# Normalised attention and a GELU layer on one core: batch 0's steps in another order and on other engines

## The chip, the cores and the metric

The kernel runs on one core of a Trainium2 chip. The metric is the device time of one execution in microseconds; the time before is the median of 3 runs. One further execution was profiled; its trace is what the views below are read from.

## The reference

q, k and v have 8 batches, 12 heads, 448 positions and 64 elements a head; the two weights are 768 x 2048 and 2048 x 768.

```
q_n = q / sqrt(mean(q*q) + 1e-6) * g_q;  k_n likewise with g_k
attn = softmax(q_n @ k_n.T / 8);  o = attn @ v
x = o, heads side by side: (8*448) x 768
h = x @ w_in;  g = gelu_tanh(h);  out = g @ w_out
```

## The kernel before

The kernel goes through the batches one after the other. While the attention of one batch runs, the second layer of the batch before it fills TensorE; the order of the later batches is written out in strings (STEPS, L641). The change touches only what comes ahead of these: the attention and the first layer of batch 0, mixed with the first steps of batch 1. That part is the string FRONT (L897), and `front` (L805) carries out its words one by one. The order of the words is the order of the instructions in each engine's queue: no scheduler moves them. An engine takes its instructions in that order and waits at each for what it needs, so a word that waits holds back every later word of the same engine, and of no other.

A word is a step, a number and, behind a colon, the engine: A ScalarE, D VectorE, P GpSimd. The heads are worked on in pairs; a chunk c is two pairs (hp 2c and 2c+1), three chunks make a batch. For batch 0 the number of the steps up to the copies is the pair.

- sq, sk: squares of the raw q or k of a pair (L175; q of 112 x 512, k of 128 x 384 for an even pair and 128 x 512 for an odd one). They are kept in the buffer that later holds g. tq, tk: their sums (L203, VectorE). rs, rS: the reciprocal root as a logarithm and an exponential (L206, ScalarE), for one pair or for both of a chunk.
- nq, nk: raw times reciprocal root, to bf16 (L220). tpq, tpk: transposes on TensorE into PSUM (L232). cq, ck: copies from there into qT and kT (L252, L258); ck multiplies by the gains, gcol.
- gcol, shift: the gains, and a bound that is taken off the scores ahead of the exponential (L780, L788).
- s: the scores of one tile (L301), of which a chunk has seven: three key blocks of the even pair, a tile "r" of the left-over keys of both pairs, three of the odd pair. e: its exponential (L332, ScalarE), which frees the PSUM place of the tile. There are two such places, and a third from U on, when the places of the transposes are given up. They are handed on first in, first out, and the "hh" tiles of the first layer take turns in the same three.
- sa, sb: the sums of a pair's exponentials by a matmul with ones, in two halves (tile o). st, rc, rb: their reciprocals (VectorE). xa, xb: exponentials times v (tile ox). xt: their product, xT (L399).
- mb, ma, mc, md: matmuls of the first layer (L504) by ranges of the six pairs; for ma to md the number i stands for columns 2i and 2i+1 of sixteen, for 7 and 8 for one column each. mb n takes pair n for columns 0 and 1, ma pairs 0 to 3, mc pair 4, md 0 to 2 pair 5, md from 3 on all six pairs. g: the GELU of a tile (L525), which frees its place.
- GELU, EXP: load of ScalarE's tables. y: matmuls of zeros, whose result nobody reads.
- L11, L12: loads of q and k of batch 1's chunks 1 and 2 on the SP queue. v, V: loads of v for batch 0 and 1; w: quarters of w_in; o: quarters of w_out. These go out on GpSimd's queue, whose DMAs take eight completion flags in turn, so that an issue waits for the landing of the eighth before it.
- Sq, Sk, Tq, Tk, Rs, Nq, Nk, Tp, Cq, Ck: the same first steps for batch 1, where Sq, Sk, Tq, Tk take a whole chunk (Sq2 is all of chunk 2's q, Sk2 its k), Rs0 makes the roots of chunks 0 and 1, and Nq01 is chunk 0, second pair. Tp0 and Tp1 transpose pairs 0 and 1 into the two single banks that the last two first-layer tiles (md7, md8) use too; pairs 2 and 3 follow behind FRONT.

Behind FRONT come the second layer of batch 0 (tiles o, mm, om; L432) and the attention of batch 1, both in the order of STEPS. Its second group of matmuls begins with the second half of w_out's columns.

The loads of q and k go out on SP's queue: three chunks of batch 0 and the first of batch 1 ahead of FRONT (L740 to L744), then L11 and L12.

Of the kernel before, what the change touches and what calls it, by code (L numbers as in the profile page):

```python
# [16 lines left out]
def kernel(  # L17
# [12 lines left out]
    B, H, S, D = q.shape  # L30
# [8 lines left out]
    P = 112  # L39
# [48 lines left out]
    gcol = consts.tile([128, 1], F32)  # L88
# [3 lines left out]
    shift = consts.tile([128, 1], F32)  # L92
# [189 lines left out]
    exs, exrs, ess, oas = {}, {}, {}, {}  # L282

    def place(name):
        i = unused.pop(0)
        t = spots[i].tile([128, 2, 512], F32, tag="sc", name=name)
        taken.append((t, i))
        return t

    def leave(t):  # L290

        n = next(n for n, (u, _) in enumerate(taken) if u is t)
        unused.append(taken.pop(n)[1])
# [7 lines left out]
    def scores(b, hp, t, parts=1):  # L301

        c, j = hp // 2, hp % 2
        sc = place("sc")
        if t == "r":
            exrs[b, c] = exr.tile([128, 2, S], BF16, tag="exr", name="exr")
            for a in range(2):
                for jj in range(2):
                    r = slice(a * D, (a + 1) * D)
                    o = slice(64 * jj, 64 * jj + 64)  # L310
                    nc.tensor.matmul(  # L311
                        sc[o, a, :S], kT[r, c, NK, o], qT[b][r, 2 * c + jj],
                        start=True, stop=True,
                    )
            dst = exrs[b, c]
        else:
            if t == 0:
                exs[b, hp] = exq.tile([128, NK, 2, S], BF16, tag="ex", name="ex")

            m = 128 // parts  # L320
            for a in range(2):
                r = slice(a * D, (a + 1) * D)
                for i in range(parts):
                    o = slice(i * m, i * m + m)
                    nc.tensor.matmul(  # L325
                        sc[o, a, :S], kT[r, c, 4 * j + t, o], qT[b][r, hp],
                        start=True, stop=True,
                    )
            dst = exs[b, hp][:, t]

        def exp():
            nc.scalar.activation(dst, sc[:, :, :S], AF.Exp, scale=scale, bias=shift)  # L332
            leave(sc)
        return exp
# [327 lines left out]
    def run(b, text, m2, call, after):  # L662

        w = work.setdefault(b, dict(n=0, a=0, but=(), k={}))
        for token in text.split():
# [5 lines left out]
            elif kind == "s":  # L671
                n = w["n"]
                if n % 3 == 0:
                    call("side", n // 3)
                scores(b, *(SEQ if n < 14 else LAST)[n], 2)()
                w["n"] += 1
                if n % 3 == 2:
# [127 lines left out]
    def front(step):  # L805
# [25 lines left out]
        elif name == "shift":  # L831
            shifts()
        elif name == "s":
            exps[i] = scores(0, *TILES[i])
        elif name == "e":
            exps[i]()
# [58 lines left out]
            raise ValueError(step)  # L895

    FRONT = """  # L897
        sk0:D v1 sq0:A tq0 tk0 rs0 gcol sk1:A sq1:D nq0:P v2 tq1 nk0:D tk1 rs1 sq2:A sk2:A tpq0
        y1 tpk0 v0 nq1:P ck0:D shift cq0:D s0 sq3:A e0 y3 s1 tq2 tq3 tk2 nk1:P L11 e1 y3 tpk1
        tpq1 s2 sk3:P w0 e2 ck1:D cq1:D tk3 y1 y1 s3 y3 y4 s4 sa0 rS1 nq2:P e3 sk4:A e4 sq4:D  # L900
        nk2:D s5 sb0 tpq2 s6 tpk2 tq4 tk4 st0 cq2:D rc0 ck2:D e5 sq5:P nk3:P nq3:D L12 e6 sa1 s7
        tpk3 tpq3 s8 sb1 e7 rs4 s9 xa0 sk5:P ck3:D rb0 cq3:D tk5 st1 e8 e9 xb0 s10 xt0 tq5 rc1
        rb1 nk4:P nq4:P e10 sa2 s11 rs5 e11 nk5:P nq5:P w1 xa1 sb2 xb1 s12 tpk4 tpq4 s13 Sq0:P
        Sk0:P e12 cq4:A st2 xt1 ck4:D rc2 rb2 e13 xa2 xb2 sa3 tpq5 tpk5 s14 e14 xt2 ck5:D cq5:D
        s15 xa3 sb3 e15 U xb3 s16 s17 s18 e16 st3 e17 rc3 rb3 xt3 e18 sa4 mb0 mb1 sb4 xa4 xb4
        s19 s20 Tq0 st4 rc4 rb4 sa5 mb2 Sk1:P w2 w3 e19 e20 GELU o0 Sq1:A xt4 Tk0 mb3 xa5 sb5
        xb5 ma1 mc0 mc1 st5 o1 V0 V1 rc5 rb5 xt5 Tq1 Tk1 Sk2:D md0 md1 ma2 mc2 md2 g0 g1 EXP md3
        Rs0 Nk00:D Nq01:D Nq00:D md4 Tp0 g2 g3 V2 o2 o3 Cq0:A g4 Nk01:D Ck0:A md5 Tp1 Nk11:D
        Nq11:D Nk10:D Nq10:D Sq2:D Tk2 Tq2 Ck1:A g5 Cq1:A md6 md7 g6 g7 md8 g8
"""  # L910
    for step in FRONT.split():
        front(step)
# [173 lines left out]
```

## Time and profile before

| | us |
|---|---|
| median of 3 runs | 407.01 (406.73 to 408.34) |
| the profiled execution | 404.76 |
| its span in the trace | 403.0 |
| TensorE busy | 392.5 (97%) |
| ScalarE busy | 304.6 (76%) |
| VectorE busy | 247.4 (61%) |
| GpSimd busy | 131.9 (33%) |

PE is TensorE, ACT ScalarE, DVE VectorE, POOL GpSimd, SP the queue that issues most DMAs. In the page's slices the span is cut into 40 of equal length, 10.1 us each; a digit is the busy share in tenths, 9 for nine tenths or more. A row of a timeline is: start, duration, engine, line, operation, written tile and read tiles with their shapes, how often; in brackets the idle time before it and what ended it. The duration of one instruction holds its way through the engine; several in a row stand closer than that, and the time of one is then the row's duration by the count. A row of DMA issues has the size and the time from issue to landing. The chain of work that ended last is followed back from the last instruction to what released it, and so on.

### The profile page before, as it was taken

Reading aid. Unit: us, or ns where it says so; the run is one execution under the profiler, and the core shown is the slowest. Engines: PE = TensorE matmul, PEld = TensorE weight load, DVE = VectorE, ACT = ScalarE, POOL = GpSimd, SP = SyncE. Lnnn points to the kernel's source line nnn. Section 1 sums busy time; section 2 is a strip of 40 time slices with the busy share of each in tenths; the row PEclk is TensorE's granted clock in tenths of the full one; section 3 lists DMA queues with packets and bytes.
Section 4 is the critical chain, followed back from the end, with each engine's and each line's share of the span. In section 5 each row is a group of like instructions: output and inputs, shape, how many; then the busy total and the mean of one; then the engine's idle time right before and its main releaser. Section 6 shows DMA issues by size and latency. Waiting matters only on the chain.

```text
span 403.0 us, 17090 instructions
## 1 busy us (share of the span) xinstructions
PE 392.5 (97%) x7632; PEld 271.7 (67%) x7632; DVE 247.4 (61%) x414; ACT 304.6 (76%) x412; POOL 131.9 (33%) x143
## 2 busy tenths in 40 slices
PE   6899999999999999999999999999999999999996
PEld 3444557667778897767867777666877667766564
DVE  5889839986987346963787426874587331880010
ACT  4997889969997689876997669876998548964400
POOL 6888000242500934065500735037500640000000
PEclk9999999999999999999999999999999999999999
DMA  7999999999990899339971399828780290210022
GB/s 186 219 227 229 205 197 200 214 251 166 214 180 3 180 190 199 76 86 199 197 127 40 78 195 191 144 53 182 135 136 15 76 144 3 81 42 2 3 78 79
DMA packets 97897, 54.64 MB, mean 136 GB/s; under 512 B 63776, under 2 KB 94368, under 8 KB 97824
## 3 DMA queue, kind: packets, MB, share of 16 engines
q1 hardware_dynamic: 71392, 41.69, 46.4%
q0 software_dynamic: 26112, 11.80, 23.1%
q8 instruction: 59, 0.97, 1.1%
q14 instruction: 14, 0.11, 0.1%
q10 hardware_dynamic: 320, 0.07, 0.1%
HBM read 45.61 MB, written 11.01 MB: 141 GB/s over the span
## 4 chain that ended last, share of the span: by engine, by line
PE 81%; DMA 6%; POOL 4%; DVE 4%; issue 2%; ACT 1%; SPq 1%; ACTq 0%; DVEq 0%; POOLq 0%
PE hh L432 23%; PE om L432 14%; PE o L432 10%; PE mm L432 10%; PE sc L325 6%; PE o L546 5%; PE hh L517 4%; PE so L432 4%; DMA vb<-in_v_dram 3%; POOL nrmq L227 1%; PE ox L371 1%; DMA rawq<-in_q_dram 1%; DVE es L346 1%; PE sc L311 1%; DMA kT<-nrmk 1%
## 5 line engine op out<-in xcount | busy, mean ns | idle before, releaser
L332 ACT ACTIVATE ex<-sc,shift 128x896 bf16<-128x896 f32 x144 | 137.7, 1016 | 8.6 <-PE sc L325 8.3
L432 PE MATMUL hh<-xT,win 64*64 64x448 bf16 x2304 | 131.7, 349 | 0.0
L432 PEld LDWEIGHTS <-g 64*64 64x64 bf16 x3072 | 103.0, 107 | 28.7 <-issue 2.2
L432 PEld LDWEIGHTS <-win 64*64 64x64 bf16 x2688 | 89.6, 107 | 37.1 <-ACTq L441 6.8
L432 PE MATMUL om<-wout,g 64*64 64x384 bf16 x1664 | 101.3, 323 | 0.2 <-issue 0.2
L432 PE MATMUL o<-wout,g 64*64 64x384 bf16 x704 | 83.4, 323 | 0.6 <-ACT g L526 0.6
L432 PE MATMUL mm<-wout,g 64*64 64x384 bf16 x704 | 83.5, 323 | 0.0
L204 DVE TENSOR_REDUCE ss<-sq 128x14 f32<-128x896 f32 (+4 forms) x45 | 47.9, 1080 | 45.4 <-ACT sq L187 37.9
L526 ACT ACTIVATE g<-hh 128x896 bf16<-128x896 f32 x55 | 49.7, 915 | 24.7 <-PE hh L432 22.8
L325 PE MATMUL sc<-qT,kT 64*64 64x448 bf16 (+1 forms) x540 | 53.7, 352 | 1.6 <-DVE qT L256 1.3
L926 POOL COPY mark<-es 1x1 bf16<-1x1 bf16 x8 | 1.8, 225 | 138.2 <-DVE xT L402 41.8
L227 POOL TENSOR_TENSOR nrmq<-rawq,rinv 112x512 bf16<-112x512 f32 x35 | 37.1, 1075 | 11.2 <-ACT rinv L213 7.4
L346 DVE TENSOR_TENSOR es<-ex 128x896 bf16<-128x896 bf16 x42 | 26.2, 624 | 21.1 <-ACT ex L332 20.8
L227 POOL TENSOR_TENSOR nrmk<-rawk,rinv 128x512 bf16<-128x512 f32 (+1 forms) x34 | 32.0, 956 | 2.0 <-ACT rinv L213 1.5
L432 PE MATMUL mm<-xT,win 64*64 64x448 bf16 x192 | 32.4, 349 | 0.0
L432 PE MATMUL o<-xT,win 64*64 64x448 bf16 x192 | 32.3, 349 | 0.0
L325 PEld LDWEIGHTS <-kT 64*64 64x64 bf16 (+1 forms) x540 | 22.4, 105 | 12.0 <-issue 4.7
L346 DVE TENSOR_TENSOR es<-es,ex 128x896 bf16<-128x896 bf16 x42 | 25.9, 616 | 4.9 <-PE mm L432 2.3
L189 POOL TENSOR_TENSOR sq<-rawq 112x1024 f32<-112x1024 f32 x8 | 15.1, 1892 | 32.7 <-DMA rawq<-in_q_dram 22.8
L280 DVE TENSOR_SCALAR kT<-kT,gcol 128x896 bf16<-128x896 bf16 x19 | 15.7, 826 | 15.4 <-DMA kT<-nrmk 15.4
L332 ACT ACTIVATE exr<-sc,shift 128x896 bf16<-128x896 f32 x24 | 24.5, 1023 | 0.1
L386 DVE STREAM_TRANSPOSE rb<-rc 128x448 f32<-128x448 f32 x36 | 23.2, 645 | 1.2
(118 smaller groups left out, 515.3 us busy)
## 6 DMA issues: line engine op xcount, KB each, us to landing
rawq<-in_q_dram SPq DMA_DIRECT2D x48, 224.0 KB, 4.7
rawk<-in_k_dram SPq DMA_DIRECT2D x48, 192.0 KB, 4.8
vb<-in_v_dram POOLq DMA_DIRECT2D x8, 576.0 KB, 8.7
win<-in_moe_w_in_dram POOLq DMA_DIRECT2D x4, 768.0 KB, 10.6
wout<-in_moe_w_out_dram POOLq DMA_DIRECT2D x4, 768.0 KB, 19.9
out_dram<-osb SPq DMA_DIRECT2D x7, 336.0 KB, 3.5
out_dram<-osb SPq DMA_DIRECT2D x8, 288.0 KB, 2.8
out_dram<-osb SPq DMA_DIRECT2D x8, 240.0 KB, 2.5
```

The source lines that it names most:

```text
L189: eng.tensor_mul(sq, raw, raw)
L204: nc.vector.reduce_sum(stat(ssq[b % 3], b, c, n, j), view(n, sqs[n, b, c], j), axis=AX.X)
L227: eng.tensor_mul(dst.rearrange("p t a d -> p a t d"), view(n, raws[n, b, c], j), r.to_broadcast(list(r.shape) + [D]),)
L280: nc.vector.tensor_scalar(kT[:, c], kT[:, c], gcol[:, 0:1], None, op0=ALU.mult)
L325: nc.tensor.matmul(sc[o, a, :S], kT[r, c, 4 * j + t, o], qT[b][r, hp], start=True, stop=True,)
L332: nc.scalar.activation(dst, sc[:, :, :S], AF.Exp, scale=scale, bias=shift)
L346: nc.vector.tensor_add(es, ex[:, 0] if t == 1 else es, ex[:, t])
L386: nc.vector.transpose(oas["rb", hp], oas["rc"].to_broadcast([128, S // 32, 32]))
L432: self.last = nc.tensor.matmul(self.outs[k][own(m)], w, e, start=not self.begun[k], stop=self.left[k] == 0,)
L517: nc.tensor.matmul(h[i * m:(i + 1) * m, j, :S], win[:, c // 2 + NCH * (c % 2), f * 128 + i * m:f * 128 + (i + 1) * m], xT[b][:, c], start= ...
L526: nc.scalar.activation(g[:, fs[0]:fs[0] + len(fs), (b % 2) * S:(b % 2 + 1) * S], hs1[fs[0]][:, :, :S], AF.Gelu_apprx_tanh)
L546: nc.tensor.matmul(o[j * m:(j + 1) * m, :HD], g[:, f, i * 128 + j * m:i * 128 + (j + 1) * m], wout[:, f, half * HD:(half + 1) * HD], start ...
```

## The change

The string FRONT is replaced by another with the same steps in another order; some of the squares, normalisations and copies of batch 0 and batch 1 name another engine. Besides, the tile of a pair's exponentials is allocated at the first of its score tiles that is issued, and no longer at tile 0, since the new order begins with tile 1.

```
--- before.py
+++ after.py
@@ -314,7 +314,7 @@
                     )
             dst = exrs[b, c]
         else:
-            if t == 0:
+            if (b, hp) not in exs:
                 exs[b, hp] = exq.tile([128, NK, 2, S], BF16, tag="ex", name="ex")
 
             m = 128 // parts
@@ -895,18 +895,18 @@
             raise ValueError(step)
 
     FRONT = """
-        sk0:D v1 sq0:A tq0 tk0 rs0 gcol sk1:A sq1:D nq0:P v2 tq1 nk0:D tk1 rs1 sq2:A sk2:A tpq0
-        y1 tpk0 v0 nq1:P ck0:D shift cq0:D s0 sq3:A e0 y3 s1 tq2 tq3 tk2 nk1:P L11 e1 y3 tpk1
-        tpq1 s2 sk3:P w0 e2 ck1:D cq1:D tk3 y1 y1 s3 y3 y4 s4 sa0 rS1 nq2:P e3 sk4:A e4 sq4:D
-        nk2:D s5 sb0 tpq2 s6 tpk2 tq4 tk4 st0 cq2:D rc0 ck2:D e5 sq5:P nk3:P nq3:D L12 e6 sa1 s7
-        tpk3 tpq3 s8 sb1 e7 rs4 s9 xa0 sk5:P ck3:D rb0 cq3:D tk5 st1 e8 e9 xb0 s10 xt0 tq5 rc1
-        rb1 nk4:P nq4:P e10 sa2 s11 rs5 e11 nk5:P nq5:P w1 xa1 sb2 xb1 s12 tpk4 tpq4 s13 Sq0:P
-        Sk0:P e12 cq4:A st2 xt1 ck4:D rc2 rb2 e13 xa2 xb2 sa3 tpq5 tpk5 s14 e14 xt2 ck5:D cq5:D
-        s15 xa3 sb3 e15 U xb3 s16 s17 s18 e16 st3 e17 rc3 rb3 xt3 e18 sa4 mb0 mb1 sb4 xa4 xb4
-        s19 s20 Tq0 st4 rc4 rb4 sa5 mb2 Sk1:P w2 w3 e19 e20 GELU o0 Sq1:A xt4 Tk0 mb3 xa5 sb5
-        xb5 ma1 mc0 mc1 st5 o1 V0 V1 rc5 rb5 xt5 Tq1 Tk1 Sk2:D md0 md1 ma2 mc2 md2 g0 g1 EXP md3
-        Rs0 Nk00:D Nq01:D Nq00:D md4 Tp0 g2 g3 V2 o2 o3 Cq0:A g4 Nk01:D Ck0:A md5 Tp1 Nk11:D
-        Nq11:D Nk10:D Nq10:D Sq2:D Tk2 Tq2 Ck1:A g5 Cq1:A md6 md7 g6 g7 md8 g8
+        sq0:D sk0:A y1 y4 tq0 tk0 sq1:D rs0 nq0:D v1 nk0:P tpk0 tpq0 gcol tq1 v2 sk1:A ck0:A cq0:D
+        tk1 rs1 s1 shift v0 sq2:P e1 nk1:D sk2:P y3 s0 tpk1 s2 e0 nq1:D ck1:D tpq1 sq3:P cq1:D y1
+        s3 sa0 e2 s5 e3 sk3:A tq2 s4 tk2 tq3 sb0 y3 L11 w0 e4 tk3 sq4:P st0 rS1 s6 sk4:P sq5:P y1
+        nq2:D e6 rc0 nk2:D e5 tpq2 sa1 nq3:P nk3:P tq4 tpk2 cq2:A ck2:A sb1 tk4 y3 s8 st1 rs4 e8
+        s7 tpk3 nk4:P rb0 sk5:P tq5 L12 e7 tpq3 s9 cq3:D nq4:P ck3:D xa0 tk5 e9 rs5 xb0 s10 rc1
+        sa2 xt0 tpk4 ck4:D e10 rb1 tpq4 s11 xa1 xb1 nk5:P sb2 nq5:P e11 Sq0:P s13 cq4:D xt1 e13
+        st2 s12 tpk5 tpq5 sa3 w1 s15 e12 Sq1:P xa2 xb2 rc2 rb2 w2 cq5:D s14 e15 ck5:D U s16 w3 xt2
+        sb3 st3 rc3 s17 xa3 e14 xb3 e17 e16 rb3 xt3 sa4 s19 mb0 o0 mb1 sb4 Tq0 o1 st4 e19 rc4 s18
+        e18 s20 e20 xa4 Sq2:A GELU V0 xb4 V1 V2 mb2 rb4 xt4 ma1 Sk0:A Tq1 sa5 sb5 xa5 Sk1:D st5
+        xb5 rc5 mb3 mc1 ma2 rb5 xt5 md1 o2 mc0 g1 Tk1 mc2 Tk0 md0 g0 Sk2:P EXP md2 md3 Rs0 o3
+        Nq00:P Nk00:P md4 Nq01:P Tq2 g2 Tp0 Tk2 Nk01:P Ck0:A Cq0:A md5 g4 Tp1 md6 Ck1:A g3 Cq1:A
+        md8 g5 Nk10:P Nq10:P md7 Nk11:P Nq11:P g6 g8 g7
 """
     for step in FRONT.split():
         front(step)
```

Counted by engine: the squares of batch 0 are on A 6, D 3, P 3 before and on A 3, D 2, P 7 after. Its normalisations are on D 3, P 9 before and on D 5, P 7 after. Its copies are on A 1, D 11 before and on A 3, D 9 after. Of batch 1, Sq1 was on A, Sk2 and Sq2 on D and the other three on P; after, Sk0 and Sq2 are on A, Sk1 on D, Sq0, Sq1 and Sk2 on P. Its eight normalisations were on D and are on P. The words y stand in other places; the DMAs of each queue keep their order.

## Prediction

> **What bounds the kernel now.** I read the page's slices first, then the chain of work that ended last for the first 75 us, then the timeline of each engine over that stretch, because every edit lies in the first 54 us.
>
> ```profile
> span 403.0 us, 17090 instructions
> PE   6899999999999999999999999999999999999996
> DMA  7999999999990899339971399828780290210022
> ```
>
> TensorE is full from the third slice on, and the DMA engines are full from the second to the twelfth. So there are two limits: TensorE's own list of work, and the moment at which data lands. The chain tells which one holds where:
>
> ```profile
> 9.30 11.74 DMA vb<-in_v_dram
> ...
> 21.09 0.95 PE ox L371 x8
> ...
> 35.73 9.94 PE hh L517 x52
> ...
> 51.01 2.29 PE h L517 x12
> ```
>
> Until 21.04 the chain is the load of v; from 21.09 to 53.30 it is TensorE nearly without a hole, the last 17.6 us of it the first layer (L517, 9.94/52 = 0.191 us a matmul). What is behind 53.3 (batch 1) starts from there. So the change gains what it brings that end forward, if nothing behind it then waits for something else, and it loses what it puts in front of TensorE. ScalarE's timeline holds the rest:
>
> ```profile
> 8.05 0.63 ACT L187 ACTIVATE g<-rawk 128x512 f32<-128x512 f32 x1 [0.62 <-DMA rawk<-in_k_dram]
> ...
> 11.85 2.79 ACT L332 ACTIVATE ex<-sc,shift 128x896 bf16<-128x896 f32 x3
> ...
> 34.87 1.28 ACT L885 ACT_TABLE_LOAD   x1
> 36.16 1.06 ACT L187 ACTIVATE sq<-rawq 112x1024 f32<-112x1024 f32 x1
> 38.52 1.73 ACT L526 ACTIVATE g<-hh 128x896 bf16<-128x896 f32 x2 [1.30 <-PE hh L517]
> 40.27 1.28 ACT L885 ACT_TABLE_LOAD   x1
> 41.56 0.34 ACT L210 ACTIVATE lg<-ss,eps 128x60 f32<-128x60 f32 x1
> 41.94 0.25 ACT L213 ACTIVATE rinv<-lg 128x60 f32<-128x60 f32 x1
> ```
>
> Exps run from 11.85 to 34.87, where the table load begins, about 0.93 us each (2.79/3), with other ScalarE work and short holes between them; then table load, a square, gelus 0 and 1, table load, batch 1's root. Two of three "hh" places are freed by those two gelus.
>
> **The change part by part.** By instructions, TensorE gets the same list in another order, ScalarE as many as before (three squares of batch 0 less, one of batch 1 and two copies more), VectorE ten less, GpSimd ten more. The edit of L317 allocates a tile at its first use and costs nothing.
>
> *The beginning.* In the old order the first normalisation sits on GpSimd, and the first copies are late behind VectorE's sums.
>
> ```profile
> 6.65 2.01 POOL L227 TENSOR_TENSOR nrmq<-rawq,rinv 112x512 bf16<-112x512 f32 x1 [2.46 <-ACT rinv L213]
> ...
> 15.28 1.41 POOL L227 TENSOR_TENSOR nrmq<-rawq,rinv 112x512 bf16<-112x512 f32 x1 [0.60 <-ACT rinv L213]
> ...
> 20.66 0.83 POOL L227 TENSOR_TENSOR nrmk<-rawk,rinv 128x384 bf16<-128x384 f32 x1 [0.53 <-DMA rawq<-in_q_dram]
> 21.45 1.04 POOL L227 TENSOR_TENSOR nrmq<-rawq,rinv 112x512 bf16<-112x512 f32 x1
> ...
> 25.96 0.88 POOL L766 DMA_DIRECT2D win<-in_moe_w_in_dram  x1
> 26.86 1.91 POOL L189 TENSOR_TENSOR sq<-rawq 112x1024 f32<-112x1024 f32 x1
> ```
>
> ```profile
> 15.22 0.56 DVE L227 TENSOR_TENSOR nrmk<-rawk,rinv 128x384 bf16<-128x384 f32 x1
> ```
>
> In the new one ck0 stands on ScalarE behind sk1, whose input lands at 8.05: 8.05 + 0.63, and about as long for the copy: 9.3; then the root rs1 (0.34 + 0.25), with the first score and the shift beside it on other engines: first exp at **9.9**, some 1.9 us earlier. From there ScalarE has 21 exps (19.5), three more roots (3 x 0.59), sk3 (0.63), cq2 and ck2 (about 1.1): 23.0, so its last exp ends near **33** instead of 34.87. The v load is issued at 8.3 to 8.6 (behind nk0 instead of nq0) and should land at 20 to 20.5. TensorE's list from the first ox to the end of md2 is the same in both; before it ends at 35.73 + 28 x 0.191 = 41.1. With the first ox 0.7 earlier and about 0.8 of waits for exps gone, I place it at **39.6**. The sum below only needs it before 41.3.
>
> *The new wait.* This decides it. In the old order ScalarE squares batch 1's second q chunk there (Sq1), which lies ready, and VectorE does the third (Sq2) later, beside the first layer. In the new order ScalarE's first step after the last exp is **Sq2**, the whole third q chunk, and its second half is nearly the last thing that the load queue brings:
>
> ```profile
> 28.21 0.38 SPq L119 DMA_DIRECT2D rawq<-in_q_dram  x1
> ```
>
> ```profile
> rawq<-in_q_dram SPq DMA_DIRECT2D x1, 224.0 KB, 8.8
> ```
>
> So it lands at 28.21 + 8.8 = **37.0**, about 4 us after ScalarE arrives. The DMA engines are full from the second slice of 10 us to the twelfth (the DMA row above), the loads ahead of this one are the same, and so an earlier front end does not bring it forward. Its bounds are one weight part of the other queue more or less ahead of it, 3.85 us (rival D has the working): 33.2 to 40.9. I take 37.0, the row itself, since the bytes ahead are the same. Behind Sq2 in ScalarE's queue stand the gelu table, Sk0, gelus 1 and 0, the exp table and batch 1's root Rs0. Who waits for them: md3 for the place that gelu 1 frees, and GpSimd's eight normalisations for Rs0. One more row is wanted, for Sk0:
>
> ```profile
> 86.26 0.95 ACT L187 ACTIVATE sq<-rawk 128x896 f32<-128x896 f32 x1
> ```
>
> The sum: 37.0 + 1.06 (Sq2) + 1.28 (table) + 0.95 (Sk0) + 0.92 (gelu 1) + 0.1 for handovers = 41.35. TensorE, done with md2 at 39.6, stands still for about 1.7 us, then md3 and md4, 24 x 0.191 = 4.6: **45.95**, against 35.73 + 9.94 = 45.67 before. The lead is gone, and 0.28 with it.
>
> *Normalisations of batch 1 on GpSimd.* Gelu 0 ends at 41.35 + 0.82 = 42.2, table 1.28, root 0.63: 44.1. Then Nq00 1.04 and Nk00 0.83: 46.0, when TensorE comes to Tp0 at 45.95. VectorE did them before, and the cover is md3 and md4 in both; now there is none to spare. Gelu 2 (44.1 + 1.28 + 0.92 = 46.3) frees md5's place as Tp0 ends. Nq01 and Nk01 are ready at 47.9, Tp1 wants them at 48.6. Nk10 to Nq11 end near 52, before the layer does, and are wanted behind it. Md6, md8 and md7 find their places free by 0.3 us or more, and the last PE matmul of the layer ends **0.3 us later than before, 53.6**.
>
> *Queues passed.* GpSimd issues the w_in and w_out loads in the same order. After the v load's issue, from 9.5 on, it has ten multiplies of 512 (1.04), three of 384 (0.83), w0 (0.88) and Sq0 (1.91), 15.7 in all, and perhaps three of them slowed by 0.4 like the one at 15.28: w1 goes out near 26.4 (25.96 before). Sq1 behind it then waits for its data:
>
> ```profile
> 19.68 0.32 SPq L119 DMA_DIRECT2D rawq<-in_q_dram  x1
> ```
>
> ```profile
> rawq<-in_q_dram SPq DMA_DIRECT2D x1, 224.0 KB, 10.0
> ```
>
> ```profile
> 32.50 1.71 POOL L766 DMA_DIRECT2D win<-in_moe_w_in_dram  x2
> ```
>
> That is 19.68 + 10.0 = 29.7, plus 1.91: w2 goes out near 31.6 instead of 32.50, and the weights land as before within half a microsecond. The last w_out part stands behind Sk2 and waits, as before, for w2's landing:
>
> ```profile
> 41.50 0.88 POOL L772 DMA_DIRECT2D wout<-in_moe_w_out_dram  x1 [2.32 <-DMA win<-in_moe_w_in_dram]
> ```
>
> ```profile
> wout<-in_moe_w_out_dram POOLq DMA_DIRECT2D x1, 768.0 KB, 22.8
> ```
>
> ```profile
> 64.19 1.01 PE L432 MATMUL om<-wout,g 64*64 64x384 bf16 x20
> ```
>
> It lands at 41.50 + 22.8 = 64.3; the third of those five steps, at 64.19 + 0.32 = 64.5, is the first to read it. So even a front end that came 1.5 us early would stand there: a gain is capped near **0.2 to 0.5 us**. SP issues the same list in the same order.
>
> [...] The slowed rows above (1.41 and 2.01 where 1.04 is usual) lie beside VectorE multiplies from SBUF, as 15.28 beside 15.22. [...]
>
> The load of 28.21 shares the engines with w2, and the row gives 8.8 us with w2 issued 4.3 us behind it. [...]
>
> **The sum.** The profiled execution took 404.76 (span 403.0, 1.8 around it), 2.25 under the median of 407.01. Plus 0.3 on either: 405.1, and against the median **407.4**. "Within 0.5%", which is about what a measurement can tell from no change, is 405.0 to 409.0.
>
> **Rivals.**
> A. *Forecast*, chance 0.60: the load holds ScalarE, 407.0 to 408.2.
> B. *The lead survives*, 0.17. If w1, issued later, lets the q load pass and it lands at 35.3 or sooner, ScalarE's chain is off the path and TensorE ends near 52. Then w_out's landing at 64.3 caps it: 406.5; if that moves as well, by up to 1.5: 405.5. For it: w1 goes out later. Against it: all bytes ahead of that load are the same.
> C. *GpSimd is too slow*, 0.10. At 1.41 for each of the four normalisations Tp0 waits 0.7 longer and Tp1 again: 408.4. Against it: VectorE's work there is sums.
> D. *The q load is overtaken by w2*, 0.13, the slower side. A weight part takes 3.85 us when that queue has the engines alone: w2 lands at 32.5 + 8.7 = 41.2,
>
> ```profile
> win<-in_moe_w_in_dram POOLq DMA_DIRECT2D x1, 768.0 KB, 8.7
> ```
>
> and from there to 64.3 six such parts pass (w3, v and the four of w_out): 23.1/6. Every microsecond that the load is later costs one, since gelu 1 is on TensorE's path from 36.7 on: 408.4 to 411.2. The kernel is slower by over 0.5% when the load lands after 38.7.
> That the order is not what the text says is excluded: the order of each engine in the built program has Sq2 ahead of the gelu table.
>
> **How the numbers follow.** Forecast 407.4. The range 405.9 to 409.3 takes A and C whole, most of B and D's first microsecond. Faster by over 0.5% needs B with both landings early and more: 0.03. Slower by over 0.5% is D's larger part and a corner of C: 0.11. Within: 0.86.
>
> **What would show it.** First exp near 9.9; last exp near 33; ScalarE idle for about 4 us before the 112x1024 square, released by rawq's DMA; TensorE idle for 1.5 to 2 us before a first-layer matmul, released by gelu 1; end of the layer at 53.6; no hole at 64. Wrong if ScalarE does not wait there, if md2 ends after 41.3, or if the transposes of batch 1 wait for GpSimd by more than 0.5 us.

## The result, and the profile after

The kernel after takes 408.36 us (median of 22 executions, 406.0 to 411.44), the kernel before, beside it, 406.72 (22 executions, 403.99 to 408.74): a ratio of 1.0045, 95% interval 1.0025 to 1.0066. That is 1.6 us slower, inside the range on record (405.9 to 409.3) and inside "within 0.5%". But the forecast came to its small loss by a mechanism that did not take place. The profiled execution of the kernel after took 408.19 us, near its median; that of the kernel before took 404.76, some 2 us under its own, so the two profiles differ by more than the kernels do. Executions that were over 1.5% above the fastest of their kernel are left out of the ratios and the means below, though not out of the medians.

The page of the kernel after, its head and two rows of the slices:

```profile
span 406.4 us, 17095 instructions
...
PE   8899999999999999999999999999999999999996
PEclk9699999999999999999999999999999999999999
```

The span is 3.4 us longer. The digit 6 in the clock row is new: in the second slice TensorE ran partly at half its clock. (Before, this row is all nines.)

To find the place, cut both spans at two marks that stand in both programs: the first ox and the end of the first layer (L517). The view of busy time by stretches has the stretch, its length, then the busy time of PE, PEld, DVE, ACT and POOL with the number of instructions, the granted clock, the DMA share and GB/s. The kernel before:

```profile
4.04:14.28 10.24, 7.36 (x53) 3.56 (x52) 8.04 (x18) 6.40 (x14) 7.37 (x8) 1.00 1.16 217
14.28:21.09 6.81, 6.16 (x52) 2.63 (x51) 6.50 (x14) 6.75 (x12) 5.69 (x6) 1.00 1.31 235
21.09:53.28 32.19, 32.15 (x232) 15.78 (x233) 25.86 (x42) 26.53 (x34) 17.00 (x17) 1.00 1.24 218
```

The kernel after:

```profile
4.00:13.23 9.23, 7.53 (x43) 3.49 (x41) 8.00 (x14) 6.16 (x13) 6.86 (x8) 1.00 1.19 225
13.23:20.06 6.83, 6.77 (x35) 2.25 (x35) 5.59 (x11) 4.64 (x8) 4.96 (x6) 0.50 1.27 247
...
23.38:55.61 32.23, 32.23 (x236) 15.45 (x235) 19.94 (x33) 26.96 (x34) 25.11 (x25) 1.00 1.26 207
```

From the first ox to the end of the layer both take 32.2 us, TensorE busy for all of it. So the wait for Sq2, the normalisations on GpSimd and everything else that the prediction weighed behind the first ox cost nothing. The first ox itself is late: 23.38 instead of 21.09, 2.3 us. In the row of 13.23 to 20.06 the granted clock is 0.50, and TensorE, busy all the time, got through 35 matmuls where the kernel before did 52 in as long. Of the 3.4 us between the two spans 2.3 are there at the layer's end; the other 1.1 lie behind it, which is less than executions of one kernel differ by (406.0 to 411.44), and was not followed. These are differences of one profile each; between the medians there are 1.6 us.

ScalarE's timeline of the kernel after shows how the beginning went:

```profile
10.62 2.98 ACT L332 ACTIVATE ex<-sc,shift 128x896 bf16<-128x896 f32 x3
14.96 1.01 ACT L332 ACTIVATE exr<-sc,shift 128x896 bf16<-128x896 f32 x1 [1.37 <-PE sc L311]
15.87 0.62 ACT L187 ACTIVATE g<-rawk 128x512 f32<-128x512 f32 x1
16.71 1.01 ACT L332 ACTIVATE ex<-sc,shift 128x896 bf16<-128x896 f32 x1 [0.22 <-PE sc L325]
17.61 0.31 ACT L210 ACTIVATE lg<-ss,eps 128x30 f32<-128x30 f32 x1
...
18.75 1.91 ACT L332 ACTIVATE ex<-sc,shift 128x896 bf16<-128x896 f32 x2 [0.57 <-PE sc L325]
20.55 0.53 ACT L254 COPY qT<-tp 128x448 bf16<-128x448 bf16 x1
...
22.03 2.81 ACT L332 ACTIVATE ex<-sc,shift 128x896 bf16<-128x896 f32 x3
```

The same stretch of the kernel before:

```profile
14.61 0.32 ACT L210 ACTIVATE lg<-ss,eps 128x30 f32<-128x30 f32 x1
...
15.10 0.99 ACT L332 ACTIVATE exr<-sc,shift 128x896 bf16<-128x896 f32 x1
...
16.40 3.69 ACT L332 ACTIVATE ex<-sc,shift 128x896 bf16<-128x896 f32 x4
```

Follow the lead. The first exp is 1.2 us earlier (10.62 against 11.85). The fourth, tile r's, is only 0.1 earlier (14.96 against 15.10), after 1.37 of waiting for its scores. The eighth, the first of chunk 1, is 2.9 later: 22.03 against 16.40 + 3 x 0.9 = 19.1. Chunk 1's root is the 128x30 row: it went from 14.61 to 17.61, 3.0 later, and from root to eighth exp it is about 4.5 in both. ScalarE used to do three of chunk 1's squares ahead of the first exp (9.89 to 11.94); now it begins the exps there, and chunk 1's sums and its last square (15.87) come later. In these two profiles the lead of the first exp goes with a late root; early_root below tests whether the root alone is the cause.

Where the lead goes is in VectorE's timeline of the kernel after:

```profile
10.61 1.18 DVE L227 TENSOR_TENSOR nrmk<-rawk,rinv 128x512 bf16<-128x512 f32 x1
11.71 1.52 DVE L227 TENSOR_TENSOR nrmq<-rawq,rinv 112x512 bf16<-112x512 f32 x1
```

and in GpSimd's, beside it:

```profile
10.42 0.81 POOL L189 TENSOR_TENSOR g<-rawk 128x384 f32<-128x384 f32 x1
11.21 1.48 POOL L189 TENSOR_TENSOR g<-rawq 112x512 f32<-112x512 f32 x1
```

TensorE's timeline of the kernel after waits for both results and falls to half clock there:

```profile
11.85 0.40 PE L246 MATMUL tp<-ident,nrmk 128*128 128x128 bf16 x4 [0.90 <-DVE nrmk L227]
...
13.29 0.56 PE L239 MATMUL tp<-ident,nrmq 112*128 112x112 bf16 x4 [0.75 <-DVE nrmq L227]
```

### The profile page after: what moved, and what is told of

Same layout as the page of the kernel before. It is cut to its first block, busy times and chain, and to the rows that moved or that the text cites. A ratio compares the mean times of both kernels' runs of the same rounds, so it can differ in the third digit from the quotient of the medians.

```text
span 406.4 us, 17095 instructions
## 1 busy us (share of the span) xinstructions
PE 396.7 (98%) x7632; PEld 271.3 (67%) x7632; DVE 246.0 (61%) x404; ACT 305.7 (75%) x412; POOL 141.1 (35%) x153
## 4 chain that ended last, share of the span: by engine, by line
PE 90%; ACT 5%; SPq 1%; DVE 1%; DMA 1%; issue 1%; ACTq 0%; DVEq 0%
PE hh L432 27%; PE om L432 16%; PE mm L432 11%; PE o L432 11%; PE sc L325 7%; PE o L546 5%; PE so L432 4%; PE hh L517 4%; ACT ex L332 3%; PE o L371 1%; PE sc L311 1%; PE ox L371 1%; DMA rawk<-in_k_dram 1%; ACT L1048 1%; PE h L517 1%
## 5 line engine op out<-in xcount | busy, mean ns | idle before, releaser
L432 PEld LDWEIGHTS <-win 64*64 64x64 bf16 x2688 | 88.1, 107 | 38.3 <-ACTq L441 6.9
L227 POOL TENSOR_TENSOR nrmq<-rawq,rinv 112x512 bf16<-112x512 f32 x37 | 38.4, 1051 | 12.7 <-ACT rinv L213 7.5
L227 POOL TENSOR_TENSOR nrmk<-rawk,rinv 128x384 bf16<-128x384 f32 (+1 forms) x38 | 36.0, 962 | 3.3 <-ACT rinv L213 2.3
L325 PEld LDWEIGHTS <-kT 64*64 64x64 bf16 (+1 forms) x540 | 22.7, 105 | 11.2 <-issue 5.1
L189 POOL TENSOR_TENSOR sq<-rawq 112x1024 f32<-112x1024 f32 x9 | 17.1, 1894 | 32.2 <-DMA rawq<-in_q_dram 28.5
L280 DVE TENSOR_SCALAR kT<-kT,gcol 128x896 bf16<-128x896 bf16 x19 | 17.0, 900 | 16.3 <-DMA kT<-nrmk 16.3
```

The lines of the kernel that those rows point to most:

```text
L189: eng.tensor_mul(sq, raw, raw)
L227: eng.tensor_mul(dst.rearrange("p t a d -> p a t d"), view(n, raws[n, b, c], j), r.to_broadcast(list(r.shape) + [D]),)
L280: nc.vector.tensor_scalar(kT[:, c], kT[:, c], gcol[:, 0:1], None, op0=ALU.mult)
L325: nc.tensor.matmul(sc[o, a, :S], kT[r, c, 4 * j + t, o], qT[b][r, hp], start=True, stop=True,)
L432: self.last = nc.tensor.matmul(self.outs[k][own(m)], w, e, start=not self.begun[k], stop=self.left[k] == 0,)
```

## The experiments

Theories to be told apart, numbered as in the expectations:

1. The forecast's: Sq2's wait for the last q load holds ScalarE, and so TensorE.
2. The half clock in the beginning (0.50 from 13.23 to 20.06, next to TensorE's two holes of 0.90 and 0.75 us) is the loss.
3. VectorE's multiplies beside GpSimd's (both read two inputs) are slowed (the 1.18 and 1.52 us above), and with them the first transposes.
4. The order leaves too little to cover chunk 1's chain from its root to its first exp.

All ratios are to executions of the kernel before on the same chip, with their 95% intervals:

| run | median us | ratio | first ox | layer end | half clock |
|---|---|---|---|---|---|
| after | 408.36 | 1.0045 (1.0025 to 1.0066) | 23.38 | 55.61 | 13.23 to 20.06 |
| again | 409.19 | 1.0016 (0.9982 to 1.0051) | 22.94 | 55.18 | 13.96 to 17.37 |
| busy | 409.50 | 1.0059 (1.0023 to 1.0095) | 24.24 | 56.46 | 20.77 to 24.18 |
| no_overlap | 408.18 | 1.0012 (0.9981 to 1.0043) | 23.55 | 55.68 | 15.15 to 21.97 |
| norms_D | 408.54 | 1.0011 (0.9983 to 1.0039) | 23.21 | 55.44 | 13.99 to 17.41 |
| order_only | 411.17 | 1.0104 (1.0073 to 1.0135) | 24.02 | 58.21 | 19.23 to 22.64 |
| engines_only | 415.05 | 1.0191 (1.0156 to 1.0226) | 27.87 | 63.01 | 13.13 to 23.37 |
| turns | 408.63 | 1.0040 (1.0014 to 1.0067) | 24.12 | 56.35 | 20.35 to 23.76 |
| before_again | 407.79 (one) | - | 20.08 | 52.27 | none |
| early_root | 408.92 | 1.0048 (1.0018 to 1.0077) | 25.23 | 57.47 | 18.47 to 25.30 |
| grafted | 407.62 | 1.0040 (1.0013 to 1.0068) | 22.70 | 56.26 | 11.83 to 18.66 |
| w1_early | 407.26 (one) | - | 22.40 | 54.78 | none |
| late_graft | 407.15 | 0.9986 (0.9962 to 1.0010) | 22.44 | 55.33 | 10.82 to 14.23 |

The last three columns are of one profiled execution each; a dash stands where there was no other execution to form a ratio from. Most intervals are some 0.3% to either side, so a ratio alone seldom decides; the rows do.

**again**: the kernel after, unaltered.

> The changed kernel, unaltered, once more. Theory 1 (the forecast's: Sq2 waits on ScalarE for the load of q): the profile of another execution shows that wait, 3 us or more ahead of the 112x1024 square, and a first layer that ends near 53.6. [...] Theory 3 (VectorE's and GpSimd's multiplies side by side are slow, and that alone makes the first pair late): nq0, nk1 and nq1 on VectorE take 1.2 to 1.5 us each in every execution, whatever the clock. Ratio to the kernel before 1.003 to 1.006.

Its median was 409.19, the ratio 1.0016, and the interval overlaps that of the first measurement between 1.0025 and 1.0051. The stretch at half clock was half as long (3.41 us), and the first ox 0.44 earlier. VectorE's two multiplies took 1.57 and 0.68 here instead of 1.18 and 1.52. So neither the stretch nor the slowed row is the same in every execution, and one profile of this kernel does not price them.

**busy**: 15 more matmuls of zeros, ahead of the two transposes that wait.

```
-s0 tpk1 s2 e0 nq1:D ck1:D tpq1
+s0 y8 tpk1 s2 e0 nq1:D ck1:D y7 tpq1
```

> The changed kernel with 15 more matmuls of zeros in TensorE's two holes ahead of tpk1 and tpq1. They compute nothing that is used. Theory 2: granted clock 1.00 throughout, first ox near 22, ratio 0.998 to 1.001, 1.5 us or more under the changed kernel. Theory 3: the clock may stay up, but the multiplies stay at 1.2 to 1.5 us and the time within 0.5 us of the changed kernel's, ratio 1.003 to 1.006. Theory 1: no difference to the changed kernel.

The clock stayed full until 20.77, past the stretch in question, and the eighth exp came no earlier. ScalarE's timeline of busy:

```profile
22.58 2.80 ACT L332 ACTIVATE ex<-sc,shift 128x896 bf16<-128x896 f32 x3 [0.69 <-PE sc L325]
```

That is 22.58 against 22.03. As the whole of the loss, theory 2 falls; the added matmuls take some TensorE time themselves, and a stretch at half clock still came at 20.77, so this does not say that the clock costs nothing. The cleaner evidence is w1_early below, whose clock was full all the way.

**no_overlap**: the multiplies of GpSimd that lay beside VectorE's first normalisations go to ScalarE.

```
-v0 sq2:P e1 nk1:D sk2:P y3 s0       +v0 e1 sq2:A nk1:D y3 s0
-tpq1 sq3:P cq1:D y1 s3 sa0 e2 s5    +tpq1 cq1:D y1 s3 sa0 e2 sk2:A sq3:A s5
-w0 e4 tk3 sq4:P                     +e4 tk3 sq4:P w0
```

> The changed kernel with the squares sq2, sk2 and sq3 on ScalarE behind its first exps instead of on GpSimd, so that GpSimd computes nothing beside nk1 and nq1 on VectorE; w0 is issued behind sq4. Theory 3: nk1 and nq1 fall to 0.6 to 0.7 us, tile r's exp comes 1.3 us earlier than in the changed kernel, first ox near 21.5, ratio 0.998 to 1.002. Theory 2: faster only if the profile shows no half clock; with shorter holes it should show none, and the ratio is the same 0.998 to 1.002; a half clock beside fast multiplies would give 1.002 or more. Theory 1: no difference to the changed kernel.

VectorE's timeline of no_overlap:

```profile
10.23 0.69 DVE L227 TENSOR_TENSOR nrmk<-rawk,rinv 128x512 bf16<-128x512 f32 x1
10.84 0.68 DVE L227 TENSOR_TENSOR nrmq<-rawq,rinv 112x512 bf16<-112x512 f32 x1
...
18.29 1.25 DVE L227 TENSOR_TENSOR nrmk<-rawk,rinv 128x384 bf16<-128x384 f32 x1
```

The same two instructions took 0.69 and 0.68 instead of 1.18 and 1.52; the third, still beside a GpSimd multiply, kept 1.25. So the slowing itself is shown. But the eighth exp began at 22.20, after 0.87 of waiting for its scores, although the root of chunk 1 came 0.7 earlier (16.93): ScalarE has three squares more ahead of that root, and the clock was at a half from 15.15 to 21.97. Which of these took the gain is not shown. The ratio lies in the range of theory 3, but the kernel after has 1.0016 on the same chip (again), so it decides nothing.

**norms_D**: batch 1's eight normalisations on VectorE, as before the change.

```
-Nq00:P Nk00:P ... Nk01:P ... Nk10:P Nq10:P ... Nk11:P Nq11:P
+Nq00:D Nk00:D ... Nk01:D ... Nk10:D Nq10:D ... Nk11:D Nq11:D
```

> The changed kernel with batch 1's eight normalisations on VectorE again. The forecast's second term (they have no cover on GpSimd): TensorE stops wanting for them at Tp0, 0.2 to 0.4 us faster than the changed kernel, ratio 1.002 to 1.006. Theories 2 and 3: what is lost is lost before 24 us, so no difference to the changed kernel by more than 0.3 us, ratio 1.003 to 1.006.

By stretches, norms_D from its first ox on:

```profile
23.21:55.44 32.23, 32.23 (x236) 15.48 (x235) 24.63 (x42) 27.00 (x34) 17.51 (x17) 1.00 1.26 211
```

Again 32.23 us, TensorE without a hole, 7.6 us of work (25.11 to 17.51) taken off GpSimd. These normalisations on GpSimd cost TensorE nothing in these profiles.

**before_again**: the kernel before, unaltered.

> The kernel before, unaltered, for a second profile. Theory 2 (the clock): no half clock ahead of the first ox, which comes at 21.1 as in the first profile; if a half clock shows here too and the first ox stays near 21.1, the clock is not what separates the kernels. Theories 3 and 4 (side-by-side multiplies; the order): first ox 21.1 and first layer's end 53.3, each within 0.4 us, whatever the clock.

Its layer ended at 52.27, a whole microsecond sooner than in its first profile, and yet this execution took 407.79. One place that gave it back stands in its groups by line between 56 and 75 us:

```profile
L432 PE MATMUL om<-wout,g 64*64 64x384 bf16 x176 | 10.8, 323 | 1.2 <-DMA wout<-in_moe_w_out_dram 1.2
```

TensorE came to the second half of w_out's columns early and waited 1.2 us for w_out's last part, which landed at 65.2. This is the cap that the prediction set for gains.

**order_only** and **engines_only**: the new order with the old engines, and the old order with the new engines, word by word; the first line of each against the kernel it starts from:

```
-sq0:D sk0:A y1 y4 tq0 tk0 sq1:D rs0 nq0:D v1 nk0:P tpk0 tpq0
+sq0:A sk0:D y1 y4 tq0 tk0 sq1:D rs0 nq0:P v1 nk0:D tpk0 tpq0

-sk0:D v1 sq0:A tq0 tk0 rs0 gcol sk1:A sq1:D nq0:P v2 tq1 nk0:D
+sk0:A v1 sq0:D tq0 tk0 rs0 gcol sk1:A sq1:D nq0:D v2 tq1 nk0:P
```

> The changed kernel's order, with every engine as in the kernel before. Theory 4: the loss is here, a hole of 1 us or more on ScalarE ahead of chunk 1's first exp, first ox 22.5 or later, ratio 1.003 to 1.006. Theory 3: multiplies at 0.55 to 0.8 us on VectorE, first ox 21.1 to 21.8, ratio 0.999 to 1.002.

> The kernel before in its own order, with every square, normalisation and copy of batches 0 and 1 on the engine that the changed kernel names. Theory 3 (VectorE's and GpSimd's multiplies side by side): the loss is here, nq0, nk1, nq1 or nk2 on VectorE take 1.2 us or more, first ox 22.5 or later, ratio 1.003 to 1.006. Theory 4 (the order: chunk 1's root stands behind the fifth exp instead of the third, so that too few exps are left to cover chunk 1's normalisation, transposes and copies): little is lost, first ox 21.1 to 21.8, ratio 0.999 to 1.002.

Each alone is worse than both together: 1.0104 and 1.0191 against 1.0045, and worse than any theory had expected. TensorE's timeline of engines_only has two holes of 2.8 us:

```profile
11.87 0.36 PE L325 MATMUL sc<-qT,kT 64*128 64x448 bf16 x2 [2.76 <-DVE qT L256]
...
16.22 0.61 PE L246 MATMUL tp<-ident,nrmk 128*128 128x128 bf16 x4 [2.85 <-DVE nrmk L227]
```

VectorE's timeline of engines_only has what comes ahead of the second:

```profile
13.80 1.15 DVE L204 TENSOR_REDUCE ss<-g 112x8 f32<-112x512 f32 x2 [1.39 <-POOL g L189]
14.86 1.29 DVE L227 TENSOR_TENSOR nrmk<-rawk,rinv 128x512 bf16<-128x512 f32 x1
```

In the old order VectorE's sums wait for squares that GpSimd now makes, and its normalisation stands behind these sums. So neither half of the change carries the loss by itself: the engines fit the new order only, the order fits the new engines better than the old, and the pair is still a little worse than the old pair.

**turns**: GpSimd does not multiply beside VectorE's normalisations. A copy of one element makes it wait for nq1 ahead of sq2, sk2 and sq3, and for nk2 ahead of nq3 and nk3.

```
-v0 sq2:P e1 nk1:D sk2:P y3 s0 ... nq1:D ck1:D ... sa1 nq3:P nk3:P
+v0 e1 nk1:D y3 s0 ... nq1:D hq sq2:P sk2:P ck1:D ... sa1 hk nq3:P nk3:P
```

> The changed kernel with GpSimd made to take turns with VectorE at two places: sq2, sk2 and sq3 wait for nq1, and nq3 and nk3 wait for nk2 (a copy of one element of their result on GpSimd, which nobody reads). Theory 3: nk1, nq1 and nk2 fall to 0.55 to 0.7 us, tile r's exp and with it the first ox come 1 us or more earlier than in the changed kernel (22.3 or sooner), ratio 0.999 to 1.003. Theory 4: the multiplies are faster but chunk 1's first exp still stands behind a hole, first ox within 0.6 us of the changed kernel's 23.4, ratio 1.002 to 1.005. Theory 2: follows the clock that the profile shows and not the multiplies.

ScalarE's timeline of turns:

```profile
13.44 1.02 ACT L332 ACTIVATE exr<-sc,shift 128x896 bf16<-128x896 f32 x1
...
22.65 2.81 ACT L332 ACTIVATE ex<-sc,shift 128x896 bf16<-128x896 f32 x3 [1.03 <-PE sc L325]
```

Tile r's exp is 1.5 us earlier than in the kernel after, and chunk 1's first exp is 0.6 later all the same. VectorE's timeline of turns says by what:

```profile
17.04 2.28 DVE L227 TENSOR_TENSOR nrmq<-rawq,rinv 112x512 bf16<-112x512 f32 x1
```

GpSimd's squares of chunk 2, pushed back behind those that waited, now lie beside nq2, which takes 2.28 instead of 0.69. Theory 3 holds for the first pair (VectorE's two multiplies took 0.69 and 0.68 here), and it is not what sets chunk 1's start; the conflict moves with the work. What four kernels (busy, no_overlap, turns, after) have in common is the eighth exp at 22.0 to 22.7, and this spoke for theory 4.

**early_root**: theory 4 put to the test: chunk 1's root is taken up to 2.2 us earlier.

```
-s3 sa0 e2 s5 e3 sk3:A tq2 s4 tk2 tq3 sb0 y3 L11 w0 e4 tk3 sq4:P st0 rS1 s6 ... nq2:D e6 rc0 nk2:D e5 tpq2
+sk3:P ... s3 sa0 e2 tq2 tk2 s5 e3 rs2 tq3 tk3 s4 sb0 y3 L11 w0 e4 nq2:D nk2:D rs3 sq4:P st0 tpq2 s6 ... tpk2 e6 rc0 cq2:A ck2:A e5
```

> The order after, but chunk 1's root is split and taken early: its last square (sk3) goes to GpSimd as in the kernel before, the sums follow at once, the first pair's root stands right behind the fourth exp, the second pair's behind the fifth, and VectorE normalises the first pair straight behind its root. Everything behind e8 stays. Theory 4 (chunk 1's chain from root to e8 has too few exps to cover it): the normalised pair is ready near 17.5, its copies near 19, e8 starts at 20 to 20.5 instead of 21.6 to 22, first ox near 21.5, the layer ends near 53.8, ratio to before 0.998 to 1.002. Theory 3 (the multiplies that VectorE and GpSimd do at the same time are the cause): sk3 on GpSimd lies beside two of VectorE's multiplies and makes these slower, e8 stays at 21.5 or later, ratio 1.003 or more. Theory 2 (the half clock): the clock still falls once in this stretch, and the time stays as in the kernel after, 1.003 to 1.005.

The root did come early, at 15.38 instead of 17.61, but the first exp of chunk 1 stood at 21.7, and the first ox at 25.23. VectorE's timeline of early_root and, behind it, TensorE's:

```profile
13.91 2.32 DVE L204 TENSOR_REDUCE ss<-g 112x8 f32<-112x512 f32 x4
16.15 1.66 DVE L227 TENSOR_TENSOR nrmq<-rawq,rinv 112x512 bf16<-112x512 f32 x1
```

```profile
17.87 0.37 PE L239 MATMUL tp<-ident,nrmq 112*128 112x112 bf16 x4 [1.08 <-DVE nrmq L227]
...
20.55 0.56 PE L325 MATMUL sc<-qT,kT 64*128 64x448 bf16 x2 [1.39 <-ACT kT L263]
```

VectorE was still adding sums until 16.15, then its multiply was slowed (1.66 instead of 0.69), and the transposes and copies that I had moved up now stood ahead of a score and an exp that lay ready. The chain from root to eighth exp took 6.3 us instead of 4.4, its last 3.3 at half clock (from 18.47). So "the root is late" describes the kernel after, but taking the root early in this way does not cure it: theory 4 in that simple form falls. A form that moves nothing ahead of ready work was not tried.

**grafted**: the kernel before's words up to its first ox, then the kernel after's remaining words in their order.

```
 ... s8 sb1 e7 rs4 s9 xa0
-sk5:P ck3:D rb0 cq3:D tk5 st1 e8 e9 xb0 s10 xt0 tq5 rc1
+st1 e8 nk4:P rb0 sk5:P tq5 cq3:D nq4:P ck3:D tk5 e9 rs5 xb0 s10 rc1 sa2 xt0 ...
```

> The order and engines of the kernel before up to its first ox, and from there the kernel after's: Sq2 behind the last exp, batch 1's normalisations on GpSimd, w1 and w2 where the kernel after has them. If all of the loss lies ahead of the first ox (theory 4, and what the two traces show), first ox at 20 to 21, layer end at 52.3 to 53.3, ratio to before 0.998 to 1.002. If the forecast's wait only stayed away because the kernel after came late (the last exp at 36 finds the load landed), it comes back here: the last exp ends near 34, Sq2 waits until the load lands at 35 or later, TensorE stands for 1 us or more behind md2, layer end 53.5 or later, ratio 1.001 to 1.006. If w1, issued later than in the kernel before, lets the q load pass (rival B), the load lands at 32 to 33.5 and Sq2 does not wait here either.

1.0040, and the seam is to blame for part: ck3 now stands behind rb0, tq5 and cq3 on VectorE. TensorE's timeline of grafted:

```profile
25.00 0.38 PE L311 MATMUL sc<-qT,kT 64*64 64x448 bf16 x4 [1.36 <-DVE kT L265]
```

So the run does not answer its first question. The load landed at 33.5 here and Sq2, at 36.9, did not wait. The run does show something else: up to the first ox its instructions are those of the kernel before, but the clock was at a half from 11.83 to 18.66, and the first ox came at 22.70 instead of 20.08 and 21.09, at full clock.

**w1_early**: the kernel after with one weight load earlier in GpSimd's order.

```
-xb1 nk5:P sb2 ... sa3 w1 s15
+xb1 w1 nk5:P sb2 ... sa3 s15
```

> The kernel after with one weight load moved: w1 goes out ahead of the last two normalisations on GpSimd, near 25.3 instead of 29.2, so that it is about 2 us ahead of the last q load in issue, as in the kernel before. If the place of w1 decides when that load lands (rival B's premise), it lands at 35.5 to 37.5 instead of 32 to 33 and Sq2, which ScalarE reaches at 36.2, waits 0 to 1.3 us; gelu 1 has 2.3 us of its own wait for TensorE to hide that, so the layer ends as in the kernel after, near 55.5. If the landing goes by bytes ahead alone (the forecast's working), it lands where it did in the kernel after, at 32 to 33.5.

With w1 issued at 24.0 instead of 29.20 the last q load landed at 36.25 instead of 32.11: the place of that one issue moves the landing by 4.1 us. ScalarE's timeline of w1_early:

```profile
36.34 1.06 ACT L187 ACTIVATE sq<-rawq 112x1024 f32<-112x1024 f32 x1 [0.86 <-DMA rawq<-in_q_dram]
...
41.02 0.92 ACT L526 ACTIVATE g<-hh 128x896 bf16<-128x896 f32 x1 [1.36 <-PE hh L517]
```

Here Sq2 does wait, 0.86 us, and it costs nothing, since gelu 1 waits 1.36 for TensorE anyway. This run has a second use: up to 24 us its order is the kernel after's, and its clock was full all the way. Its eighth exp began at 21.05 and its first ox at 22.40, still 1.3 to 2.3 later than in the two full-clock profiles of the kernel before; VectorE's two multiplies took 1.61 and 1.52.

**late_graft**: the kernel before's words up to xb1, w1 among them, then the kernel after's.

```
 ... nk5:P nq5:P w1 xa1 sb2 xb1
-s12 tpk4 tpq4 s13 Sq0:P Sk0:P e12 cq4:A ...
+tpk4 ck4:D tpq4 Sq0:P s13 cq4:D xt1 e13 st2 s12 ...
```

> The kernel before's order and engines up to the step xb1, w1 at the kernel before's place among them, and from there the kernel after's: Sq2 first behind the last exp, batch 1's normalisations on GpSimd. So the lead that the forecast counted on and its late q load come together here for the first time. The forecast: first ox near 20 to 21, last exp ends near 33.5, the load lands at 36 to 37, ScalarE waits 2.5 us or more for it, gelu 1 starts at 40.4 to 41.4, TensorE waits 0.5 to 1.7 us behind md2, layer end 53.3 to 53.8. The theory that the second part costs nothing because TensorE is the bound there: ScalarE waits for the load, but TensorE does not wait for gelu 1 by more than 0.3 us, and the first layer ends 32.2 us behind the first ox, at 52.3 to 53.3. By both, the kernel after's loss is ahead of this seam, so the ratio to before is 0.998 to 1.0025; 1.004 or more would say that the second part costs as well.

0.9986 (0.9962 to 1.0010): with the old beginning the kernel after's remaining part, Sq2 first on ScalarE and batch 1's normalisations on GpSimd, is as fast as the kernel before. This is the cleanest of the runs: within that interval the loss lies ahead of the seam, in the order and engines of the beginning. ScalarE's timeline of late_graft:

```profile
36.01 1.05 ACT L187 ACTIVATE sq<-rawq 112x1024 f32<-112x1024 f32 x1
...
41.66 0.92 ACT L526 ACTIVATE g<-hh 128x896 bf16<-128x896 f32 x1 [2.33 <-PE hh L517]
```

In the profiled execution the load landed at 34.8, ahead of ScalarE, and TensorE had no hole behind the first layer's start. The wait that "decides it" in the forecast was seen in one run only, 0.86 us long, and for nothing. But no run brought ScalarE to Sq2 before 35.5, so what a wait of 4 us would cost is not shown.

The profile of late_graft is a warning too. Its first ox (22.44) and its layer end (55.33) are nearly as late as those of the kernel after, though its words up to that ox are the kernel before's. The clock was at a half from 10.82 to 14.23, and the scores of tile r came at 14.88 instead of 13.81. Then one VectorE multiply was slowed, which took 0.77 in the kernel before. VectorE's timeline and TensorE's:

```profile
19.23 1.77 DVE L227 TENSOR_TENSOR nrmq<-rawq,rinv 112x512 bf16<-112x512 f32 x1
```

```profile
21.05 0.37 PE L239 MATMUL tp<-ident,nrmq 112*128 112x112 bf16 x4 [0.99 <-DVE nrmq L227]
```

So both troubles, the half clock and the slowed multiply, can hit the old beginning as well; a single profile of a first ox near 22.4 does not tell the two beginnings apart; the ratio over the executions does.

## Why the prediction was right or wrong, point by point

**The time** was right to 1.0 us (407.4 against 408.36), by luck: as a difference 0.4 was forecast and 1.6 measured. The forecast was a lead of 1.9 us that a wait takes, and 0.28 more; what happened is that the lead did not last to the first ox, and the wait did not come either.

**"First exp at 9.9 … its last exp ends near 33 … first ox 0.7 earlier"** is the step that failed. The first exp came at 10.62, the last ended at 36.3, the first ox was 2.3 late, and md2 ended near 43.1 (Tp0, behind md4, begins at 47.70; less 24 x 0.191), where "the sum only needs it before 41.3". The work was counted rightly (23.0 us, and ScalarE was busy for 22.5), but as if ScalarE were the only bound of the beginning: its waits were put at nothing. In the kernel before that was nearer the truth, 21.6 us busy of the 23.0 between 11.85 and 34.87. In the new order it is 22.5 of 25.7 from the first exp to the end of the last, since its exps wait for scores, these for copies, transposes and normalisations. The prediction did not follow one chunk's chain (square, sum, root, normalisation, transpose, copy, score) through the new order; had it done so, it would have found the root of chunk 1 behind the fifth exp instead of the third.

**"This decides it": the load lands at 37.0, "since the bytes ahead are the same".** Wrong. (Its sums are slightly off too, without effect: the terms of 41.35 add up to 41.31, and 407.01 plus 0.3 is 407.3.) ScalarE's timeline of the kernel after:

```profile
34.40 1.91 ACT L332 ACTIVATE ex<-sc,shift 128x896 bf16<-128x896 f32 x2 [0.40 <-PE sc L325]
36.19 1.05 ACT L187 ACTIVATE sq<-rawq 112x1024 f32<-112x1024 f32 x1
...
41.85 0.92 ACT L526 ACTIVATE g<-hh 128x896 bf16<-128x896 f32 x1 [2.33 <-PE hh L517]
```

No bracket before the square: its data had been there since 32.11. It is ScalarE that waits for TensorE ahead of gelu 1, 2.33 us, not the other way round. The DMA issues of the kernel after, from 27.4 to 27.6 us:

```profile
rawq<-in_q_dram SPq DMA_DIRECT2D x1, 224.0 KB, 4.7
```

4.7 us from issue to landing, where the row on record has 8.8. And GpSimd's timeline of the kernel after:

```profile
29.20 0.88 POOL L766 DMA_DIRECT2D win<-in_moe_w_in_dram  x1
```

w1 went out 1.75 us behind that load's issue (27.45) instead of 2.25 ahead of it (25.96 and 28.21). The forecast of 26.4 was GpSimd's work added up without its waits, some 3 us of them, the same omission as on ScalarE. w1_early confirms the premise of rival B: w1's place decides the landing (36.25 against 32.11). Rival B's time did not follow, because the lead it was to preserve was not there. Rival D, the slower side, did not occur: w2 was issued at 31.94, and the load landed at 32.11.

**Normalisations of batch 1 on GpSimd**, "no cover to spare": right. 32.23 us from first ox to layer end with them on GpSimd and 32.23 with them on VectorE. They took 1.03 and 0.82, against 1.04 and 0.83 in the sum, and rival C did not occur. That they would keep the usual time beside VectorE's sums was the author's estimate, and it was not tested: VectorE's last sum had ended at 45.05 and the first of them began at 45.93, so VectorE had no work beside them.

**Multiplies side by side in the beginning** were priced on GpSimd alone ("slowed by 0.4"). VectorE's side was left at nothing, and there it was 1.18 and 1.52 against 0.69 and 0.68 (no_overlap). A slowing that both engines show was charged to one of them.

**"A gain is capped"** by w_out's last part, landing 64.3: it landed at 65.03, and TensorE came to those five steps only at 66.53; no hole, as forecast, because there was no gain. That the cap is real before_again shows (1.2 us).

**The clock** was no step of the prediction at all, since the page on record shows nines. Over the executions of the two kernels, on several chips, whose mean granted clock is on record (89 and 33), by bands of that clock:

| mean clock of the execution | before: executions, mean us | after: executions, mean us |
|---|---|---|
| 0.9975 or more | 51, 406.77 | 5, 407.56 |
| 0.9935 to 0.9975 | 15, 406.75 | 17, 408.35 |
| under 0.9935 | 23, 407.96 | 11, 409.50 |

A stretch of 3.41 us at half clock lowers the mean by 0.0042 (0.5 x 3.41/406), so by this estimate an execution under 0.9975 had 2 us or more at half clock: 38 of 89 before and 28 of 33 after. In grafted and late_graft, which begin with the old words, it was 7 of 23. So the new beginning loses the clock more often. Within one kernel an execution is longer where its clock is lower: about 150 us per unit of clock over all kernels of this study, an estimate from the executions, so about 0.6 us for one such stretch. The mean clock is 0.9964 before and 0.9943 after; 0.0021 x 150 = 0.3 us of the 1.5 between the means of these executions (407.08 and 408.61). The other 1.2 stay at equal clock. This is a correlation, not an experiment: busy, which moved the stretch to 20.77, was no faster.

**What stays open.** Shown: the loss is ahead of xb1, within the interval of late_graft; neither the new order nor the new engines can be blamed alone, since either without the other loses more (order_only, engines_only); VectorE's multiplies are slowed beside GpSimd's (1.18 and 1.52 us in the kernel after, 0.69 and 0.68 in no_overlap; 2.28 in turns, 0.69 in the kernel after); the root of chunk 1 comes 3.0 us late in the profiles compared. Not settled: how the 1.2 us at equal clock divide between the order of chunk 1's steps and the slowing, since after each remedy alone (no_overlap, turns, early_root) TensorE or ScalarE waited at another place, and none has a ratio that can be told from the kernel after's. No version here beats the kernel before by more than its interval.

## What to carry to other kernels

Adding up an engine's work gives the earliest end, not the end: where engines hand a tile around, follow one tile's whole chain through the new order and compare when its root, its copy and its first consumer come, before counting a lead. A start that comes earlier is worth only what the next tile's chain can follow; here a first exp 1.2 us sooner went with an eighth 2.9 us later. And here the landing of a load depended on what was issued ahead of it on the other queue too (4.1 us, w1_early), so the waits of the engine that issues the other queue belong in the sum.

## What the runs showed of the hardware that was not expected

- A VectorE multiply of two SBUF inputs beside a GpSimd multiply: 112x512 in 1.32 (the kernel after) to 2.28 us (turns) instead of 0.68, 128x384 in 1.25 (no_overlap) instead of 0.55; the GpSimd multiply 1.35 (the kernel after) to 2.02 (engines_only) instead of 1.04. It was not every such pair: now VectorE's, now GpSimd's row is the long one. In the kernel after each of three such rows ends a little less than its usual time behind the end of the other engine's row: VectorE's two 0.56 and 0.54 us behind (alone 0.69 and 0.68), GpSimd's of 11.21 0.90 behind (alone 1.04). What ties the two ends together is not shown.
- The stretches at half clock lasted 3.41, 6.83 or 10.24 us: one, two or three times 3.41. They began 10.8 to 20.8 us into the span, and the same beginning, the kernel before's, had none (both its profiles), one of 3.41 (late_graft) or one of 6.83 (grafted).
- TensorE's busy share in the 3.41 us just ahead went with the fall. In all eleven profiles with a stretch at half clock in the beginning, TensorE was busy for 0.97 to 2.13 us of the 3.41 before it (the kernel after: 1.82, with no hole longer than 0.90). Cut into 3.41 us from the moment the clock rose, the stretches that kept the clock held more, up to about 25 us into the span, except four of 1.87 to 2.11 (before, before_again, w1_early, grafted). Over a longer stretch the share says little: the kernel after lost its clock behind 7.53 busy of 9.23 us, the kernel before kept it behind 7.36 of 10.24.
- One 768 KB weight load issued 4 us ahead of a 224 KB load instead of 1.75 behind it made that load land 4.1 us later (36.25 against 32.11).
